# Attention, a routed mixture and a second MLP on one core: another placement for staged weight loads, conversions split into steps, another order at the end of attention

## The chip, the cores and the metric

The kernel runs on one core of a Trainium2 chip. The metric is device time in microseconds (us) of one execution; lower is better. The core's engines are TensorE (PE; its weight loads are shown apart as PEld), VectorE (DVE), ScalarE (ACT), GpSimd (POOL) and SyncE (SP), which here only issues transfers. Each engine works through its own instructions in order; an instruction that waits holds back all that stand behind it on that engine.

## The reference

Three stages, all in float32. Attention looks back over a window of 64 positions; its output goes through a mixture of 8 experts, of which each row uses the one with the largest logit (rows with a skip score of 0 or less pass through unchanged); the result goes through a second MLP with 2048 inner columns.

```python
scores = scale * q @ k.T                      # q, k, v: [4, 8, 576, 64]
mask = (rel >= 0) & (rel < 64)                # rel = pos[:, None] - pos[None, :]
attn = softmax(where(mask, scores, -1e9))
x = (attn @ v) laid out as [2304, 512]

do_compute = x @ w_skip > 0
logits = x @ w_gate                           # 8 experts
gate = softmax(logits) at the largest logit
x = x + gate * (relu(x @ w1[e]) @ w2[e])      # w1: [8, 512, 1024], w2: [8, 1024, 512]

h = x @ w_in                                  # w_in: [512, 2048], w_out: [2048, 512]
g = where(h >= 1, h, where(h <= -1, 0, (h + 1) ** 2 / 4))
out = g @ w_out
```

## The kernel before

A matrix product in full precision is made of three products of halves: every operand is split into a rounded upper half and a remainder, and three of the four cross products are summed. So each weight has to be loaded (a **raw** tile), split by ACT (copy of the upper half) and by DVE or POOL (subtraction, `split_pair`, L120), and kept in a ring of 14 pairs of split weights. A raw tile is 512 KB. The weights of the second MLP come in another number format (`in_wd`, 64-bit words); five DVE operations turn a raw tile of it into float32 first (`convert_ops`, L127: shift, two or-with-mask operations, the magnitude, a compare-and-multiply), and two converted tiles (half pairs) make one pair to split. Some are converted early (`EARLY`, kept in the pools `early` and `earlier`), the others (`LATE`, 24 half pairs) during the second MLP.

**Raw loads.** All raw loads stand in one list, `to_load`, in the order in which they are used. `load_raws` (L96) starts as many as there is room for: at most `most[0]` in flight, in three pools of 4, 2 and 2 places (the third exists from the experts on). It takes the last pool that has room, `room[-1]`. `load_raws` is called whenever a split or a conversion has taken a raw tile, so a new load often gets the place of the tile that was just taken, and its transfer waits until the engine that reads that tile is done. Raw loads are issued by SP, between its other loads.

**Attention.** 18 tiles of 128 rows go through a loop over `t` (L557), software-pipelined: `stage_v(t-3)` (probabilities times values, PSUM tile `o`; then DVE makes `den`, `rec`, `x`), `stage_t(t-2)` (transposes `pt`, copied to `pts`), `stage_s(t)` (scores `s`, from q and k; DVE `nb`, ACT `pr`), the routing of earlier tiles (`stage_l2`, `stage_l`, `stage_x` with the transposes `px`, and `route_a` to `route_c` for groups of three tiles), then from the third iteration on one split on POOL, and raw loads. `stage_v(t)` also issues the two value loads (`vt`, 130 KB each) that `stage_v(t+2)` reads; odd iterations load 512 KB each of q and k; each tile of the result is stored to `x1` (256 KB) by ACT's queue. In iterations 5 and 8 a whole conversion stands at the end of the iteration (L589). The tiles still in the pipeline after the loop are finished by hand-ordered calls (L601 to L637).

**Experts.** For each of the 8 experts one or more tiles of 128 rows are gathered, go through `ffn` and are stored back. Weights are split and converted in hooks between the matmuls.

**Second MLP.** 96 steps; step k runs `stage_h` (matmuls `h`, 12 of 384 columns, for one block of 128 inner columns) and, two steps behind, `stage_o` (matmuls `po`, 9 of 512 columns). The step's DVE and ACT work makes `gs` from `h`. `bring_at` says in which step which half pair of `LATE` is converted (between the step's own DVE operations); a pair is split at the end of the step after its second half (`split_whole`). `prep_block` transposes the input rows of a block (`p2x`) and splits them into `x2T`. Two half pairs are converted ahead of step 0 (`AHEAD_OF_IT`). Before:

```python
bring_at = {}
for n in range(AHEAD_OF_IT, len(LATE)):
    bring_at[n - AHEAD_OF_IT if n < 8 else 6 + (n - 8) * 7 // 5] = n
```

Of the kernel before, what the change touches and what calls it, by code (L numbers as in the profile page):

```python
# [10 lines left out]
F32 = mybir.dt.float32  # L11
F32R = mybir.dt.float32r
BF16 = mybir.dt.bfloat16
I32 = mybir.dt.int32
# [5 lines left out]
P = 128  # L20
# [9 lines left out]
NT = N // P  # L30
# [21 lines left out]
)  # L52
AHEAD_OF_IT = 2

# [10 lines left out]
def moe_chain(  # L65
# [30 lines left out]
    def load_raws(eng=nc.sync):  # L96
        while to_load and len(raws) < most[0]:
            used = [n for _, n in raws.values()]

            last = to_load[0] in LATE  # L100
            room = [n for n in range(1 if last else len(rawp)) if used.count(n) < RAWS[n]]
            if not room:
                return
            u, c = to_load.pop(0)
            at = rawp[room[-1]]
            if u < U_IN:
                r = at.tile([P, 2, 512], F32, tag="raw", name=f"raw{u}_{c}")
                eng.dma_start(r, wu[u, :, c : c + 2])
            else:
                r = at.tile([P, 512, 2], I32, tag="raw", name=f"raw{u}_{c}")  # L110
                eng.dma_start(
                    r.rearrange("p n w -> p (n w)").bitcast(I64), wd[u - U_IN, :, c]
                )
            raws[u, c] = r, room[-1]

# [39 lines left out]
    def do_split(u, c, eng):  # L155
        split_pair(u, c, raws.pop((u, c))[0] if u < U_IN else early.pop((u, c)), ring, eng)
        load_raws()

    def do_convert(u, c, into):
        if c % 2 == 0:  # L160
            early[u, c] = into.tile([P, 2, 512], F32, tag="early", name=f"c{u}_{c}")
        convert(early[u, c // 2 * 2][:, c % 2].bitcast(I32), raws.pop((u, c))[0])
        load_raws()

    def work(todo, engines):
# [82 lines left out]
    with ExitStack() as actx:  # L248
# [79 lines left out]
        def stage_t(t):  # L328
            for g in (2 * t, 2 * t + 1):
# [4 lines left out]
                pts = ap2.tile([P, 4, P], F32, tag="pts", name=f"pts{g}")  # L334
                if g % 2 == 0:
                    nc.scalar.activation(pts, pt, AF.Copy)
# [213 lines left out]
        nc.scalar.dma_start(x1[N : N + 1, :].rearrange("o (p c) -> (o p) c", p=27), zero)  # L550
        load_raws()
        of = {}
        for j, n in enumerate(ROUTES):
            t0 = len(of)
            of.update({t0 + i: (t0, i, n, j % 2) for i in range(n)})
        due, since = {}, {}
        for t in range(NT):  # L557
            if t >= 3:
# [10 lines left out]
            if t >= 3:  # L569
                store_t(t - 3, nc.scalar)  # L570
            if t >= 5:
                stage_l2(t - 5, *of[t - 5][1:])
# [14 lines left out]
            for f in due.pop(t, ()):  # L587
                f()
            if t in (5, 8):  # L589
                work(converts, [dve])  # L590

            if splits and since.get(splits[0][1:], t) + 2 <= t:
                work(splits, [pool])
            load_raws()
            for key in raws:
# [3 lines left out]
        t0 = t1 - ROUTES[-2]  # L599
        later = [f for g in sorted(due) for f in due[g]]  # L600
        stage_v(NT - 3)  # L601
        store_t(NT - 3, nc.scalar)
        stage_t(NT - 2)
        stage_l2(NT - 5, *of[NT - 5][1:])
        stage_l(NT - 4)
        stage_x(NT - 3)
        stage_t(NT - 1)
        stage_v(NT - 2)
        store_t(NT - 2, nc.sync)
        stage_l2(NT - 4, *of[NT - 4][1:])  # L610
        route_a(t0, of[t0][2])
        stage_l(NT - 3)
# [3 lines left out]
        end["lg"] = psp.tile([P, 4, P], F32, tag="pt0", name="lg_end")[:, 0, 0 : n * (NE + 1)]  # L616
        end["rk"] = psp.tile([P, 4, P], F32, tag="pt1", name="rk_end")
        stage_l2(NT - 3, *of[NT - 3][1:])
        for f in later:
# [15 lines left out]
        route_c(t1, n)  # L635
        work(converts, [dve] * len(converts))
        work(splits, [pool] * len(splits))  # L637
# [163 lines left out]
    with ExitStack() as fctx:  # L801
# [25 lines left out]
        def stage_h(xT, nb, m, k):  # L827
            turn[0] ^= 1
            ph = bank(6 + turn[0], [P, TB], f"h2_{nb}_{m}")
            n = 0  # L830
            for c in range(KD):
                for a, b in PASSES:
                    nc.tensor.matmul(  # L833
                        ph, lhsT=halves[U_IN + m // 4, c][:, b, (m % 4) * P : (m % 4 + 1) * P],
                        rhs=xT[:, a, c, :], start=(n == 0), stop=(n == 3 * KD - 1),
                    )
                    n += 1

# [62 lines left out]

        bring_at = {}
        for n in range(AHEAD_OF_IT, len(LATE)):
            bring_at[n - AHEAD_OF_IT if n < 8 else 6 + (n - 8) * 7 // 5] = n
        first = ring.tile([P, 2, 2, 512], F32, tag="pair", name="c_first")
# [3 lines left out]
        def half_pair(n):  # L909
# [7 lines left out]
            r = raws[u, c][0]  # L917
            mag = fp.tile([P, 512], F32, tag="mag", name=f"mag{u}_{c}")
            ops = convert_ops(cws[n // 2][:, c % 2].bitcast(I32), r, mag)
            return ops, [partial(nc.scalar.activation, mag, r[:, :, 1].bitcast(F32), AF.Abs)]  # L920

        def done(n):
            raws.pop(LATE[n])
            load_raws()
# [27 lines left out]
        xs = {0: load_block(0, nc.sync)}  # L952

        most[0] = RAWS[0] - 1
        load_raws()
# [24 lines left out]
        for k in range(len(steps) + LAG):  # L980
# [9 lines left out]
            if k >= LAG:  # L990
# [9 lines left out]
                if k < len(steps):  # L1000
                    stage_o(pos[v], gss.pop(k - LAG), m, m0, m1)
                    if m == KF - 1:
                        finish(pos[v], nb, rest=rest if v == 5 else None)
                    if HF + LAG <= k + 1 < HF + LAG + NTT:
                        put_aside(pos[0], k + 1 - HF - LAG)
# [66 lines left out]
```

## Time and profile before

| | us |
|---|---|
| median of 3 runs | 749.52 (745.4 to 752.06) |
| profiled execution, its time | 744.33 |
| its span, first to last instruction | 742.6 |
| mean granted TensorE clock in it | 0.98 of full speed |
| PE busy, of the span | 682.9 (92%) |
| DVE busy | 432.9 (58%) |
| ACT busy | 382.3 (51%) |
| POOL busy | 95.1 (13%) |

Busy shares are means over three unlike stages. Attention runs to about 146 us, the experts from there to about 306 us, the second MLP to the end. A time in brackets behind an instruction in the timeline is the idle time of its engine just before it, with what ended it. PE times in a timeline show the clock too: the same group of matmuls takes longer when the granted clock is low.

### The profile page before, as it was taken

How to read it: one execution, taken by the hardware profiler on the slowest of the kernel's cores; microseconds unless marked ns; L12 is line 12 of the kernel's file. 1: busy time of each engine (PE TensorE's matmuls, PEld its weight loads, DVE VectorE, ACT ScalarE, POOL GpSimd, SP SyncE). 2: the span in 40 equal slices, each digit the busy share in tenths (PEclk: the TensorE clock that was granted, in tenths of full speed). 3: DMA queues.
4: the chain of work that ended last, by engine and by line, in shares of the span. 5: the costliest groups of instructions: out<-in, count | busy, mean ns of one | idle time of the engine just before them, and what ended most of it. 6: DMA issues, size and time to landing. Idle time of an engine off the chain costs nothing.

```text
span 742.6 us, 12124 instructions
## 1 busy us (share of the span) xinstructions
PE 682.9 (92%) x4605; PEld 581.4 (78%) x4605; DVE 432.9 (58%) x851; ACT 382.3 (51%) x761; POOL 95.1 (13%) x96
## 2 busy tenths in 40 slices
PE   7677887789798999799899999999999999999997
PEld 6565666667676777488798998999998998998995
DVE  4477776649759159679888874434343443333332
ACT  5654663027456257356676665545444544445443
POOL 2335554322022122100000000000000000000000
PEclk9987999999999999999999999999999999999999
DMA  8896965158949348354242400202030021002001
GB/s 262 261 280 199 288 197 144 31 172 265 334 134 350 115 126 297 135 172 142 87 142 86 128 1 0 72 15 72 15 86 1 1 44 43 1 0 44 1 1 43
DMA packets 34502, 88.81 MB, mean 120 GB/s; under 512 B 6958, under 2 KB 8110, under 8 KB 34420
## 3 DMA queue, kind: packets, MB, share of 16 engines
q1 hardware_dynamic: 26208, 74.34, 32.5%
q10 hardware_dynamic: 5892, 6.83, 2.8%
q0 software_dynamic: 2320, 6.58, 2.7%
q8 instruction: 47, 0.77, 0.4%
q14 instruction: 35, 0.29, 0.1%
HBM read 75.65 MB, written 13.12 MB: 120 GB/s over the span
## 4 chain that ended last, share of the span: by engine, by line
PE 47%; DVE 7%; DMA 3%; issue 2%; ACT 2%; ACTq 0%; POOLq 0%; DVEq 0%; SPq 0%
PE po L862 23%; PE h L833 23%; DVE c L855 2%; DMA x<-mx,idx 2%; ACT q L845 1%; DVE gs L853 1%; DVE w L123 1%; DVE c L852 1%; PE p2x L824 1%; DMA mx<-x,idx 1%; DVE q L844 1%; DVE x2T L118 0%; DVE q L848 0%; PE spare L946 0%; DVE c_first L855 0%
## 5 line engine op out<-in xcount | busy, mean ns | idle before, releaser
L833 PE MATMUL h<-x2T,w 128*128 128x384 f32 x1152 | 218.2, 337 | 4.3 <-ACT x2T L117 2.2
L862 PE MATMUL po<-w,gs 128*128 128x512 f32 x864 | 217.4, 395 | 0.7 <-DVE w L123 0.6
L833 PEld LDWEIGHTS h<-x2T,w 128*128 128x128 f32 x1152 | 204.6, 188 | 13.6 <-DVE x2T L118 2.7
L862 PEld LDWEIGHTS po<-w,gs 128*128 128x128 f32 x864 | 159.5, 188 | 31.2 <-DVE w L123 1.3
L841 ACT ACTIVATE q<-h 128x384 f32<-128x384 f32 x96 | 47.0, 489 | 109.7 <-PE h L833 108.3
L844 DVE TENSOR_SCALAR q<-q 128x384 f32<-128x384 f32 x96 | 34.3, 358 | 99.9 <-ACT q L841 99.6
L848 DVE TENSOR_TENSOR q<-hs,q 128x384 f32<-128x384 f32 x96 | 53.6, 559 | 49.5 <-ACT q L845 49.5
L850 ACT ACTIVATE gs<-q 128x384 fp32r<-128x384 f32 x96 | 50.4, 525 | 60.0 <-DVE q L848 60.0
L853 DVE TENSOR_TENSOR gs<-q,gs 128x384 fp32r<-128x384 f32 x96 | 53.6, 558 | 43.8 <-ACT gs L850 43.8
L720 PE MATMUL y<-w,hT 128*128 128x512 f32 x264 | 69.3, 402 | 4.9 <-DVE hT L118 4.9
L122 ACT ACTIVATE w<-raw 128x1024 fp32r<-128x1024 f32 x64 | 65.4, 1063 | 14.1 <-PEq L779 3.6
L845 ACT ACTIVATE q<-q 128x384 f32<-128x384 f32 x96 | 50.5, 526 | 23.3 <-DVE q L844 20.1
L720 PEld LDWEIGHTS y<-w,hT 128*128 128x128 f32 x264 | 47.7, 188 | 17.4 <-DVE hT L118 8.4
L123 DVE TENSOR_TENSOR w<-raw,w 128x1024 fp32r<-128x1024 f32 x50 | 58.9, 1218 | 2.6 <-ACT w L122 1.6
L323 ACT ACTIVATE pr<-s,nb 128x128 f32<-128x128 f32 x144 | 39.1, 386 | 29.4 <-DVE nb L319 29.4
L843 ACT ACTIVATE hs<-h 128x384 f32<-128x384 f32 x96 | 46.8, 488 | 0.0
L123 POOL TENSOR_TENSOR w<-raw,w 128x1024 fp32r<-128x1024 f32 x14 | 33.4, 2387 | 62.1 <-ACT w L122 62.1
L682 PE MATMUL ha<-w,mxT 128*128 128x512 f32 x132 | 34.0, 404 | 7.8 <-DVE mxT L118 3.3
L348 PE MATMUL o<-vt,pts 128*64 128x65 f32 x576 | 27.0, 250 | 12.4 <-DMA vt<-in_vs 11.1
L682 PEld LDWEIGHTS ha<-w,mxT 128*128 128x128 f32 x132 | 23.8, 188 | 17.1 <-DVE mxT L118 4.1
L348 PEld LDWEIGHTS o<-vt,pts 128*64 128x64 f32 x576 | 23.6, 160 | 16.3 <-DMA vt<-in_vs 10.8
L682 PE MATMUL hb<-w,mxT 128*128 128x512 f32 x132 | 35.0, 401 | 0.0
(159 smaller groups left out, 702.4 us busy)
## 6 DMA issues: line engine op xcount, KB each, us to landing
raw<-in_wu SPq DMA_DIRECT2D x62, 512.0 KB, 6.4
raw<-in_wd SPq DMA_DIRECT2D x32, 512.0 KB, 4.3
x<-x SPq DMA_DIRECT2D x20, 256.0 KB, 3.3
x<-x ACTq DMA_DIRECT2D x19, 256.0 KB, 5.8
vt<-in_vs SPq DMA_DIRECT2D x36, 130.0 KB, 5.6
out<-out SPq DMA_DIRECT2D x36, 128.0 KB, 2.4
q<-in_qs SPq DMA_DIRECT2D x8, 512.0 KB, 7.4
kt<-in_ks SPq DMA_DIRECT2D x8, 512.0 KB, 8.4
```

What stands on the lines that cost most here:

```text
L122: nc.scalar.activation(t[:, 0], src, AF.Copy)
L123: eng.tensor_tensor(t[:, 1], src, t[:, 0].bitcast(F32), ALU.subtract)
L348: nc.tensor.matmul(o[k * BLK : (k + 1) * BLK, h, 0:VW], lhsT=pts[k][:, h // 2, half * BLK : (half + 1) * BLK], rhs=vt[(2 * t + k) % B][:, ...
L682: nc.tensor.matmul(ph, lhsT=xT[:, a, c, :], rhs=halves[4 * e + j, c][:, b, :], start=(n == 0), stop=(n == len(seq) - 1),)
L720: nc.tensor.matmul(py, lhsT=hT[j][:, a, c, :], rhs=halves[4 * e + 2 + j, c][:, b, :], start=(j == 0 and c == 0 and (a, b) == PASSES[0]), s ...
L833: nc.tensor.matmul(ph, lhsT=halves[U_IN + m // 4, c][:, b, (m % 4) * P : (m % 4 + 1) * P], rhs=xT[:, a, c, :], start=(n == 0), stop=(n == ...
L841: nc.scalar.activation(q, ph, AF.Relu, bias=0.5, scale=0.5)
L845: nc.scalar.activation(q, q, AF.Square)
L848: nc.vector.tensor_tensor(q, h, q, ALU.max)
L850: nc.scalar.activation(gs[:, 0], q, AF.Copy)
L853: dve.tensor_tensor(gs[:, 1], q, gs[:, 0].bitcast(F32), ALU.subtract)
L862: nc.tensor.matmul(po[i], lhsT=gs[:, a, i * P : (i + 1) * P], rhs=w[:, b, :], start=(m == m0 and (a, b) == PASSES[0]), stop=(m == m1 - 1 a ...
```

## The change

- `load_raws` picks, of the pools with room, the one from which a tile was taken longest ago (`left`, `take_raw`), no longer the last.
- No raw load stands ahead of the attention loop, and none in its iteration 0.
- The two conversions inside the loop are cut into their ten operations, two in an iteration from iteration 6 on (`convert_by_parts`): one before `stage_l2`, one behind the routing.
- After the loop, `stage_t(16)` goes ahead of `stage_v(15)`, `stage_t(17)` ahead of `stage_x(15)`, `route_a` of tiles 12 to 14 behind `stage_v(17)`; one store goes from ACT's queue to SP's; one `pts` copy goes from ACT to DVE.
- Three half pairs, not two, are converted ahead of the second MLP; for the first two the magnitude is written into a part of the ring (`first`), no longer into a new tile of the pool `fp`. The others come in steps 0, 1, 3, 4, 6, and from step 8 on three in four steps (before: one in each of steps 0 to 8, then five in seven).
- Up to four raw loads are in flight at the start of the second MLP, three from step 6 (before: three from the start). In step 0 the matmuls that read the upper half of x come first.

```diff
-AHEAD_OF_IT = 2
+AHEAD_OF_IT = 3
@@ load_raws
             u, c = to_load.pop(0)
-            at = rawp[room[-1]]
+            n = min(reversed(room), key=lambda n: left.get(n, 0))
+            at = rawp[n]
...
-            raws[u, c] = r, room[-1]
+            raws[u, c] = r, n
+
+    left = {}
+
+    def take_raw(key):
+        r, n = raws.pop(key)
+        left[n] = max(left.values(), default=0) + 1
+        return r
...
+    def convert_by_parts(todo, into):
+
+        for _, u, c in todo:
+            if c % 2 == 0:
+                early[u, c] = into.tile([P, 2, 512], F32, tag="early", name=f"c{u}_{c}")
+            for op in convert_ops(early[u, c // 2 * 2][:, c % 2].bitcast(I32), raws[u, c][0]):
+                yield
+                op()
+            take_raw((u, c))
+            load_raws()
@@ stage_t
-                if g % 2 == 0:
+
+                if g % 2 == 0 and t + 2 != NT:
                     nc.scalar.activation(pts, pt, AF.Copy)
@@ the attention loop
-        load_raws()
...
+        parts = convert_by_parts(converts, earlyp)
         for t in range(NT):
...
                 store_t(t - 3, nc.scalar)
+            if t >= 6:
+                next(parts, None)
             if t >= 5:
                 stage_l2(t - 5, *of[t - 5][1:])
...
-            if t in (5, 8):
-                work(converts, [dve])
+            if t >= 6:
+                next(parts, None)
...
-            load_raws()
+            if t:
+                load_raws()
...
+        stage_t(NT - 2)
         stage_v(NT - 3)
-        store_t(NT - 3, nc.scalar)
-        stage_t(NT - 2)
+        store_t(NT - 3, nc.sync)
         stage_l2(NT - 5, *of[NT - 5][1:])
         stage_l(NT - 4)
+        stage_t(NT - 1)
         stage_x(NT - 3)
-        stage_t(NT - 1)
         stage_v(NT - 2)
...
-        route_a(t0, of[t0][2])
         stage_l(NT - 3)
...
+        route_a(t0, of[t0][2])
         stage_l2(NT - 3, *of[NT - 3][1:])
@@ the second MLP
+            seq = [(c, a, b) for c in range(KD) for a, b in PASSES]
+            if k == 0:
+                seq.sort(key=lambda z: z[1])
...
+        bring_at = {0: 3, 1: 4, 3: 5, 4: 6, 6: 7}
+        for n in range(8, len(LATE)):
+            bring_at[8 + (n - 8) * 4 // 3] = n
...
+            if n < 2:
+
+                mag = first[:, 1, n]
+            else:
+                mag = fp.tile([P, 512], F32, tag="mag", name=f"mag{u}_{c}")
...
-        most[0] = RAWS[0] - 1
         load_raws()
...
+                    if k == 6:
+
+                        most[0] = RAWS[0] - 1
```

What stands in the engines' rows, at three places. First SP, from the first loads of q and k to the loads of iteration 5 (`raw0_0` is the raw tile of unit 0, first pair; `vt0` to `vt3` are the four value tiles, `kt` the keys). Before:

```order
L108 DMA raw0_0_244<-in_wu 128x1024
L108 DMA raw0_2_246<-in_wu 128x1024
L270 DMA q2_317<-in_qs 128x1024
L274 DMA kt_148<-in_ks 128x1024
L108 DMA raw1_0_371<-in_wu 128x1024
L108 DMA raw1_2_373<-in_wu 128x1024
L279 DMA vt0_149<-in_vs 64x520
L279 DMA vt1_150<-in_vs 64x520
L270 DMA q3_449<-in_qs 128x1024
L274 DMA kt_148<-in_ks 128x1024
L111 DMA raw32_0_463<-in_wd 128x512
L279 DMA vt2_151<-in_vs 64x520
```

And with the change, the same stretch:

```order
L290 DMA q2_313<-in_qs 128x1024
L294 DMA kt_148<-in_ks 128x1024
L110 DMA raw0_0_316<-in_wu 128x1024
L110 DMA raw0_2_318<-in_wu 128x1024
L110 DMA raw1_0_368<-in_wu 128x1024
L299 DMA vt0_149<-in_vs 64x520
L299 DMA vt1_150<-in_vs 64x520
L290 DMA q3_444<-in_qs 128x1024
L294 DMA kt_148<-in_ks 128x1024
L110 DMA raw1_2_458<-in_wu 128x1024
L299 DMA vt2_151<-in_vs 64x520
```

The first raw loads moved behind the load of `q2`, and one raw load fewer stands ahead of the first `vt0`. Before, `raw1_0` takes the place of `raw0_0`, `raw32_0` that of `raw0_2`, `raw32_1` that of `raw1_0`; with the change these three and `raw1_2` all get places that nothing has used yet, `raw2_0` and `raw2_2` the places of `raw0_0` and `raw0_2`. From iteration 8 on all six places are taken in both kernels, and most loads get the place of the tile whose split was issued in the same iteration.

Second DVE, the end of iteration 5 and the start of iteration 6 before (`c_0` is the converted tile, `xT` the copy of the transposes `px`):

```order
L393 COPY ls_642<-misc 128x128
L374 COPY xT_649<-px_644 128x512
L153 TENSOR_SCALAR c_0_651<-raw_0_463 128x512
L153 SCALAR_TENSOR_TENSOR c_0_651<-raw_0_463,c_0_651 128x512 x2
L153 TENSOR_SCALAR raw_0_463<-raw_0_463 128x512
L153 SCALAR_TENSOR_TENSOR c_0_651<-raw_0_463,c_0_651 128x512
L355 TENSOR_SCALAR den_681<-o_664 128x8
```

With the change, the end of iteration 6 and iteration 7 up to its routing:

```order
L395 COPY xT_738<-px_733 128x512
L181 TENSOR_SCALAR c_0_725<-raw_0_550 128x512
L376 TENSOR_SCALAR den_765<-o_748 128x8
L378 RECIPROCAL rec_767<-den_765 128x8
L380 TENSOR_TENSOR x_769<-o_748,rec_767 128x512
L359 COPY pts_785<-pt_780 128x512
L339 TENSOR_REDUCE nb_808<-s_788 128x4
L339 TENSOR_REDUCE nb_810<-s_789 128x4
L181 SCALAR_TENSOR_TENSOR c_0_725<-raw_0_550,c_0_725 128x512
L414 COPY ls_832<-misc 128x128
```

Five operations in a row ahead of `den` have become one ahead of `den` and one between `nb` and `ls` in each iteration.

Third DVE, from the start of the second MLP to step 0 (`c_first` holds the first converted tiles, `x2T` the split input rows). Before:

```order
L959 SCALAR_TENSOR_TENSOR c_first<-mag_1_5892,c_first 128x512
L123 TENSOR_TENSOR w_0_5900<-c_first,w_0_5900 128x1024
L118 TENSOR_TENSOR x2T_5885<-p2x_0_5903,x2T_5885 128x4x128
L118 TENSOR_TENSOR x2T_5885<-p2x_1_5912,x2T_5885 128x4x128
L118 TENSOR_TENSOR x2T_5885<-p2x_2_5921,x2T_5885 128x4x128
L844 TENSOR_SCALAR q_0_5954<-q_0_5954 128x384
L847 TENSOR_SCALAR c_first<-raw_2_5138 128x512
```

With the change:

```order
L986 SCALAR_TENSOR_TENSOR c_first<-c_first 128x512
L986 TENSOR_SCALAR c_first<-raw_2_5138 128x512
L986 SCALAR_TENSOR_TENSOR c_first<-raw_2_5138,c_first 128x512 x2
L986 SCALAR_TENSOR_TENSOR c_first<-mag_2_5900,c_first 128x512
L132 TENSOR_TENSOR w_0_5908<-c_first,w_0_5908 128x1024
L127 TENSOR_TENSOR x2T_5885<-p2x_0_5911,x2T_5885 128x4x128
L127 TENSOR_TENSOR x2T_5885<-p2x_1_5920,x2T_5885 128x4x128
L127 TENSOR_TENSOR x2T_5885<-p2x_2_5929,x2T_5885 128x4x128
L869 TENSOR_SCALAR q_0_5962<-q_0_5962 128x384
L872 TENSOR_SCALAR c_first<-raw_3_5146 128x512
```

The third half pair (`raw_2`) moved from step 0 to a place ahead of the split and of `x2T`; step 0 now converts the fourth.

## Rows read from the trace of the kernel before

**Rows 1.** Stretches of 20 us: busy us of each engine, PEclk, DMA share, GB/s

```profile
40.00:60.00 20.00, 15.36 (x222) 11.71 (x219) 14.17 (x32) 9.15 (x25) 7.14 (x3) 0.83 1.00 297
...
120.00:140.00 20.00, 15.52 (x238) 12.36 (x230) 13.72 (x53) 3.79 (x12) 4.26 (x6) 0.91 0.27 79
...
340.00:360.00 20.00, 16.05 (x80) 13.69 (x79) 18.56 (x34) 12.99 (x27) 0.00 (x0) 1.00 0.37 118
...
400.00:420.00 20.00, 20.00 (x103) 18.21 (x102) 17.09 (x32) 12.23 (x25) 0.00 (x0) 1.00 0.26 79
```

**Rows 2.** Timeline of PE in attention: start, us, line, tile, count, idle before

```profile
15.99 1.24 PE L348 MATMUL o<-vt,pts 128*64 128x65 f32 x32 [0.16 <-issue]
...
20.89 1.15 PE L348 MATMUL o<-vt,pts 128*64 128x65 f32 x32
21.98 1.09 PE L333 MATMUL pt<-ident,pr 128*128 128x128 f32 x8
...
30.31 0.35 PE L348 MATMUL o<-vt,pts 128*64 128x65 f32 x2 [4.83 <-DMA vt<-in_vs]
30.95 1.97 PE L348 MATMUL o<-vt,pts 128*64 128x65 f32 x30 [0.30 <-DMA vt<-in_vs]
...
36.50 0.66 PE L372 MATMUL px<-ident,x 128*128 128x128 f32 x4
...
44.15 1.09 PE L372 MATMUL px<-ident,x 128*128 128x128 f32 x4 [2.52 <-DVE x L359]
45.16 2.00 PE L348 MATMUL o<-vt,pts 128*64 128x65 f32 x32
...
53.00 0.33 PE L348 MATMUL o<-vt,pts 128*64 128x65 f32 x2 [1.88 <-DMA vt<-in_vs]
...
54.73 1.97 PE L333 MATMUL pt<-ident,pr 128*128 128x128 f32 x8
...
68.92 1.09 PE L372 MATMUL px<-ident,x 128*128 128x128 f32 x4 [4.05 <-DVE x L359]
...
77.01 1.15 PE L348 MATMUL o<-vt,pts 128*64 128x65 f32 x32
```

**Rows 3.** Timeline of SP in attention: start, us, loads issued in a row

```profile
22.30 0.80 SPq L108 DMA_DIRECT2D raw<-in_wu  x2
23.19 1.11 SPq L279 DMA_DIRECT2D vt<-in_vs  x2
```

**Rows 4.** SP's waits from 0 to 130 us: line, releaser, total us, times, longest

```profile
SPq L108 <- POOL w L123: 22.9, 6, 5.2
SPq L111 <- POOL w L123: 14.8, 4, 6.9
```

**Rows 5.** Timelines of DVE and POOL around the two conversions in attention

```profile
38.45 1.42 DVE L153 SCALAR_TENSOR_TENSOR c<-raw,c 128x512 int32<-128x512 int32 x2
...
40.25 2.72 DVE L153 SCALAR_TENSOR_TENSOR c<-raw,c 128x512 f32<-128x512 f32 x1
...
63.22 3.45 DVE L153 SCALAR_TENSOR_TENSOR c<-raw,c 128x512 int32<-128x512 int32 x2
...
39.92 2.50 POOL L123 TENSOR_TENSOR w<-raw,w 128x1024 fp32r<-128x1024 f32 x1 [9.03 <-ACT w L122]
```

**Rows 6.** Timeline of PE after the attention loop

```profile
132.37 0.42 PE L385 MATMUL misc<-xT,wg_sb 128*32 128x128 f32 x8 [1.84 <-DVE d L416]
```

**Rows 7.** PE's waits from 320 to 400 us: total us, times, longest

```profile
PE h L833 <- ACT x2T L117: 2.2, 1, 2.2
PE h L833 <- DVE x2T L118: 2.0, 2, 1.1
PE po L862 <- DVE w L123: 0.6, 1, 0.6
```

**Rows 8.** The chain that ended last, start of the second MLP: start, us, what

```profile
319.34 1.77 PE spare L946 x5
321.12 2.12 PE h L833 x12
```

More of the change, by code (lines that the diff above doesn't have):

```diff
@@ L155, in do_split @@
     def do_split(u, c, eng):
-        split_pair(u, c, raws.pop((u, c))[0] if u < U_IN else early.pop((u, c)), ring, eng)
+        split_pair(u, c, take_raw((u, c)) if u < U_IN else early.pop((u, c)), ring, eng)
         load_raws()
@@ L161, in do_convert @@
             early[u, c] = into.tile([P, 2, 512], F32, tag="early", name=f"c{u}_{c}")
-        convert(early[u, c // 2 * 2][:, c % 2].bitcast(I32), raws.pop((u, c))[0])
+        convert(early[u, c // 2 * 2][:, c % 2].bitcast(I32), take_raw((u, c)))
         load_raws()
+    def convert_by_parts(todo, into):
[7 more added lines that the diff above has]
+            load_raws()
     def work(todo, engines):
@@ L635, in moe_chain @@
         route_c(t1, n)
-        work(converts, [dve] * len(converts))
+        for _ in parts:
+            pass
         work(splits, [pool] * len(splits))
@@ L829, in stage_h @@
             ph = bank(6 + turn[0], [P, TB], f"h2_{nb}_{m}")
[L830 to L837, printed above, removed]
+            seq = [(c, a, b) for c in range(KD) for a, b in PASSES]
+            if k == 0:
+                seq.sort(key=lambda z: z[1])
+            for n, (c, a, b) in enumerate(seq):
+                nc.tensor.matmul(
+                    ph, lhsT=halves[U_IN + m // 4, c][:, b, (m % 4) * P : (m % 4 + 1) * P],
+                    rhs=xT[:, a, c, :], start=(n == 0), stop=(n == 3 * KD - 1),
+                )
             fill, mags, ends = bring(k)
@@ L900, in moe_chain @@
         part = dram.tile([TB, DM], F32, name="part")
-        bring_at = {}
-        for n in range(AHEAD_OF_IT, len(LATE)):
-            bring_at[n - AHEAD_OF_IT if n < 8 else 6 + (n - 8) * 7 // 5] = n
+        bring_at = {0: 3, 1: 4, 3: 5, 4: 6, 6: 7}
+        for n in range(8, len(LATE)):
+            bring_at[8 + (n - 8) * 4 // 3] = n
         first = ring.tile([P, 2, 2, 512], F32, tag="pair", name="c_first")
@@ L917, in half_pair @@
             r = raws[u, c][0]
-            mag = fp.tile([P, 512], F32, tag="mag", name=f"mag{u}_{c}")
+            if n < 2:
+                mag = first[:, 1, n]
+            else:
+                mag = fp.tile([P, 512], F32, tag="mag", name=f"mag{u}_{c}")
             ops = convert_ops(cws[n // 2][:, c % 2].bitcast(I32), r, mag)
@@ L922, in done @@
         def done(n):
-            raws.pop(LATE[n])
+            take_raw(LATE[n])
             load_raws()
```

## The prediction

> **What bounds the kernel now.** I read the stretches of 20 us first: where is PE not full, and at what clock? From 400 us on it is busy 20.00 of 20 us at full clock; there nothing of this change can win or lose. In the second MLP's first 80 us it falls to 16.05 of 20 while DVE stands at 18.56, so DVE sets the pace; in attention it is at 15.36, at a mean granted clock of 0.83, with the transfers at a share of 1.00 [rows 1].
>
> In PE's timeline of attention the reader is to see that a good iteration of the loop is short and few are good. From `o` at 15.99 to `o` at 20.89 it takes 4.90 us. The next seven, up to 77.01, take 56.12, where seven of 4.90 would be 34.3: 21.8 us too much [rows 2]. The brackets say why. Twice PE waits for value loads, 4.83 and 1.88 us, and twice for DVE's `x`, 2.52 and 4.05 us; and after each such wait the same groups take nearly twice as long (`o` 1.97 or 2.00 for 1.15, `pt` 1.97 for 1.09, `px` 1.09 for 0.66), as at 1.2 instead of 2.4 GHz [rows 2].
>
> Who holds the value loads? SP's timeline shows two raw loads at 22.30 and the two `vt` loads behind them at 23.19, though `stage_v` of that iteration, whose end frees the `vt` tile, ended at 17.2 (15.99 + 1.24) [rows 2, 3]. SP's list of waits names the blocker: raw loads waited 22.9 + 14.8 = 37.7 us in ten waits for POOL's split of the tile whose place they take [rows 4]. Who holds `x`? The conversions, of which one operation took 2.72 us, where two of its kind took 1.42 together, beside a split on POOL [rows 5].
>
> The expert stage loses its time to orders that the change leaves as they are; its splits, conversions and matmuls stand in the same order on PE, DVE, ACT and POOL, and only the places of its raw tiles are dealt out differently. I cost it at nothing; the cover is that transfers run far ahead of it (share 0.27 from 120 to 140 us) [rows 1], and if that is gone the head start is lost there (second rival).
>
> **Part 1, raw loads.** In iterations 2 to 7 the loads now get places that are fresh or were left iterations ago, so SP no longer stands at POOL there. What that frees: the waits of 4.83 and 1.88 us, and the slow groups right behind them, 1.97 − 1.15 = 0.82 and 1.97 − 1.09 = 0.88 [rows 2]: 8.4 us. From iteration 8 on all six places are taken, and loads wait for the split of their own iteration as before; I count nothing there. The raw loads that no longer stand ahead of the loop start about an iteration later, and each split with them; the splits still end inside the loop.
>
> **Part 2, conversions by steps.** The two lumps cost PE 2.52 and 4.05 us of waiting, and in slow groups 1.09 − 0.66 = 0.43 and 2.00 − 1.15 = 0.85 behind the first, and behind the second the same two and a `pt` of 1.97 − 1.09 = 0.88, as behind the wait at 53.00 [rows 2]: 10.0 us. Nothing of the work goes away: ten operations of up to 0.7 us remain, two in an iteration. What hides them is DVE's own idle time: even in the stretch with the first lump it is busy 14.17 of 20 us [rows 1]. Queued behind the one that stands ahead of `den` are `den`, `rec`, `x`, and PE's `px` behind those; about 2.0 us of lateness is free there, since the 4.5 us of the first lump from 38.45 to 42.97 made PE wait only 2.52 [rows 2, 5]. Without that cover each step would cost up to its two operations, 1.4 us.
>
> Parts 1 and 2 together would give 18.4 of the 21.8 us. But a second limit comes next: the transfers. In the seven iterations from the one at 20.89 on the changed kernel moves 11 raw tiles of 512 KB, three loads each of q and k of 512 KB, 14 value loads of 130 KB and 7 stores of 256 KB, together 12.6 MB (5.77 + 3.15 + 1.86 + 1.83). At the 297 GB/s that a full stretch showed [rows 1] that is 42.4 us, so these iterations can hardly fall below 42.4 from 56.1: at most 13.7 of the 18.4 us. Value loads queue behind raw loads in such traffic, so some waits stay. I take **11 us**, with ends of 4 (only the first wait goes, and little else) and 18 (part of the raw traffic runs over into later iterations, where the share falls).
>
> A rule of the skill speaks against part 2, and the trace shows its effect. The row: the operation of 2.72 us began at 40.25, while POOL's subtraction ran from 39.92 to 42.42; before POOL began, two such operations took 1.42 [rows 5]. The Trainium skill, "SBUF — State Buffer", section "SBUF: two separate sides", says that VectorE and GpSimd share a pair of ports as an exclusive lock, and that a VectorE operation with two inputs in SBUF fully blocks while a GpSimd operation that reads SBUF holds it; here it agrees with the row. By that rule six of the ten operations (those that read the raw tile or the magnitude and the converted tile) can each be held, at six moments instead of two; this is the third rival.
>
> **Part 3, the end of attention.** Now PE waits 1.84 us because `route_a` (started at its `d`) stands ahead of the copy `ls` on DVE [rows 6]; the new order puts it behind the last `stage_v`. The transposes moved up let their copies run while PE does `o`; the copy that goes from ACT to DVE adds one copy to DVE's queue, with `den` and PE's next `px` behind it. The group behind the wait ran slow too (0.85 at most, from `o` in attention). `route_a` itself is not gone, its operations now delay the last `ls`. Between 0 and 2.7 us; I take **2**, near the row's own wait. The store moved to SP's queue stands behind nothing but value loads; zero.
>
> **Part 4, the second MLP.** PE's waits from 320 to 400 us are 2.2 + 2.0 us for `x2T` and 0.6 us for a split, 4.8 in all [rows 7]. They come from one half pair converted in each of steps 0 to 8 with DVE at 18.56 of 20 [rows 1]; with one half pair ahead of step 0 and five in the first eight steps, these steps lose a third of their conversions, and from step 8 on three in four steps is about the old rate (five in seven) with other neighbours. So 4.8 us go. One split becomes late anew: the pair for inner block 6 is split at the end of step 7 and read in step 8, where before a whole step lay between; I price that at the one such wait that the trace has, 0.6 [rows 7]. Net **4.2 us**, between 2.5 and 5. The start itself gains nothing: PE's own keep-warm matmuls end at 321.12, and `h` follows at once [rows 8], so an earlier `x2T` and the reordered matmuls of step 0 find PE busy. The third half pair sits in the wait for the last stores of the experts, where DVE has nothing else; had it no room there, its four operations, 2.8 us (4 × 0.71 [rows 5]), would come ahead of `x2T`. Raw loads, one more of them in flight, stand behind the first block's x loads on SP.
>
> **Sum.** 11 + 2 + 4.2 = 17.2 us off the profiled execution of 744.33 (span 742.6 and 1.7 around it): 727.1. That execution was below the median of the runs, 749.52; off the median it is **732.3**, and I forecast 732.
>
> **The rivals.** *The transfers take it back.* With the stalls gone the raw loads, splits and value loads crowd into less time, and the waits for `vt` return one after another, from iteration 8 on more than now. For it: the share of 1.00 [rows 1] and the unchanged placement from iteration 8. Against: 120 to 140 us has a share of 0.27, so there is room to run over [rows 1]. Price: the loop keeps 4 us: 749.5 − 4 − 2 − 4.2 = 739.3.
>
> *The experts absorb the head start.* They begin 13 us earlier, but their first raw tiles may not be there, and ACT's splits wait for them. Against it is that idle share just before they begin [rows 1]. It would leave part 4 only: 745.3, within 1%.
>
> *Slower: the lock between DVE and POOL.* Place: iterations 6 to 11, each with two conversion operations and one split on POOL. If both of an iteration were held to 2.72 us each, 5.4 us of lateness against the 2.0 that is free makes a PE wait of 3.4, and slow groups of 0.43 + 0.85 + 0.88 = 2.2 behind it [rows 2, 5]: 5.6 in each of five iterations, 28. Against that stand the 10.0 of the two lumps, some 5 of part 1, 2 and 4.2: 749.5 + 28 − 21.2 = 756.3. It decides when four of the five iterations meet it (4 × 5.6 = 22.4). Against: one held operation in an iteration costs 2.72 − 2.0 = 0.7 and no more, and of the trace's six such operations two were held, one in each lump (2.72, and 3.45 for a pair) [rows 5].
>
> **How the numbers follow.** Forecast, gains of 11 to 22 us (727 to 738): 0.62. More than that, the loop at its bound of 18 and the other parts at theirs (down to 721): 0.06. Transfers, around 739 (738 to 742): 0.18. Experts, 742 to 747: 0.09. Lock, above 747: 0.05. The range 721 to 744 leaves out the last and about half of the one before. Faster by over 1%, which is about what a measurement of this kernel can tell (its three runs spread 0.9%), means below 742.0: 0.86; within 1%: 0.09; slower: 0.05.
>
> **What the changed profile would show.** Part 1: SP's waits of raw loads for POOL fall from 37.7 us to about half, and the wait for `vt` of 4.83 is gone. Part 2: no wait of PE for `x` above 1 us in the loop; the granted clock from 40 to 60 us rises above 0.83. The iteration that starts at 77.01 now starts near 66. Part 3: no wait of 1.84 us for `d`. Part 4: waits for `x2T` gone, one for a split of about 0.6, PE full from about 325 less the head start. The forecast is wrong if the loop's iterations stay near 8 us with the transfers at a share of 1.00, if held conversion operations pile up, or if the experts' first tiles wait for raw loads.

## Result, and the profile after

The median is 737.42 us (20 runs, 729.69 to 743.4) against 747.13 us (20 runs) for the kernel before on the same chips: a ratio of 0.9875, interval 0.9853 to 0.9897, 9.3 us less. The time lies in the range and the direction is right; the gain is little more than half of the 17.2 us forecast. The profiled execution took 739.42 us (span 737.7). It lies 2.0 us above its median, and that of before 2.8 us below the median of these runs, so stretches of the two profiles must be compared with their scatter in mind. One kernel of the study (POOL issues, with the new end) has its profile from a disturbed execution; it is left out below, and its two successors stand for it.

The windows of 20 us that answer to [rows 1] (columns as there):

```profile
20.00:40.00 20.00, 18.74 (x341) 14.49 (x340) 14.17 (x32) 15.88 (x43) 7.11 (x3) 1.00 1.02 320
40.00:60.00 20.00, 15.88 (x252) 12.01 (x252) 16.33 (x48) 12.83 (x34) 9.07 (x6) 0.90 1.05 265
...
340.00:360.00 20.00, 17.40 (x88) 14.92 (x87) 15.50 (x29) 12.35 (x25) 0.00 (x0) 1.00 0.34 105
```

From 20 to 60 us the transfers now stand at a share above 1.00; from 340 to 360 DVE fell from 18.56 to 15.50 and PE rose from 16.05 to 17.40. PE's timeline of attention, as in [rows 2]: the same iterations start at

```profile
21.92 1.15 PE L369 MATMUL o<-vt,pts 128*64 128x65 f32 x32
...
44.77 0.33 PE L369 MATMUL o<-vt,pts 128*64 128x65 f32 x2 [1.95 <-DMA vt<-in_vs]
...
65.53 1.45 PE L369 MATMUL o<-vt,pts 128*64 128x65 f32 x32
...
85.75 0.33 PE L369 MATMUL o<-vt,pts 128*64 128x65 f32 x2 [1.21 <-DMA vt<-in_vs]
...
105.54 1.53 PE L369 MATMUL o<-vt,pts 128*64 128x65 f32 x32 [1.52 <-DMA vt<-in_vs]
```

The iteration that started at 77.01 starts at 65.53 (forecast: near 66), and the seven iterations ahead of it take 43.6 us, not 56.1. The six behind it take 40.0 us (65.53 to 105.54), where before they took 37.2 (77.01 to 114.20). SP's waits for POOL tell the same story, split at that iteration, first after, then before (columns as in [rows 4]; the rows ahead of the dots are the earlier stretch):

```profile
SPq L110 <- POOL w L132: 4.8, 2, 2.8
...
SPq L110 <- POOL w L132: 15.6, 4, 7.0
SPq L113 <- POOL w L132: 7.5, 2, 5.0
```

```profile
SPq L108 <- POOL w L123: 11.2, 3, 5.2
SPq L111 <- POOL w L123: 0.3, 1, 0.3
...
SPq L111 <- POOL w L123: 14.6, 3, 6.9
SPq L108 <- POOL w L123: 6.7, 2, 4.0
```

In the earlier stretch they fell from 11.5 to 4.8 us; in the later one they stayed, 21.3 and 23.1. SP's largest wait of the earlier stretch before, which the prediction left out, was another one, for DVE; with the change it fell as well (before, then after):

```profile
SPq L108 <- DVE rec L357: 14.8, 2, 8.9
```

```profile
SPq L110 <- DVE rec L378: 3.2, 1, 3.2
```

The two waits before ended at 42.99 and 67.77, as the two conversions ended (42.97 and 67.74; the view names `rec`, which stands right behind them on DVE): each time a raw load was to take the place of the tile that was being converted. The conversions, grouped by form as busy us and mean ns, answer to [rows 5]:

```profile
L181 DVE SCALAR_TENSOR_TENSOR c<-raw,c 128x512 int32<-128x512 int32 x4 | 2.9, 717 | 0.0
L181 DVE SCALAR_TENSOR_TENSOR c<-raw,c 128x512 f32<-128x512 f32 x2 | 1.4, 682 | 0.0
```

None was held. Before:

```profile
L153 DVE SCALAR_TENSOR_TENSOR c<-raw,c 128x512 int32<-128x512 int32 x4 | 4.8, 1200 | 0.1
L153 DVE SCALAR_TENSOR_TENSOR c<-raw,c 128x512 f32<-128x512 f32 x2 | 3.4, 1706 | 0.1
```

At the end of attention the wait of 1.84 us for `d` [rows 6] is gone, and others stand in its place, in PE's timeline:

```profile
118.59 0.66 PE L393 MATMUL px<-ident,x 128*128 128x128 f32 x4 [0.32 <-DVE x L380]
121.75 0.43 PE L406 MATMUL misc<-xT,wg_sb 128*32 128x128 f32 x8 [1.10 <-DVE xT L395]
122.79 0.66 PE L393 MATMUL px<-ident,x 128*128 128x128 f32 x4 [0.61 <-DVE x L380]
126.16 0.53 PE L537 MATMUL misc<-at,to 128*128 128x144 f32 x3 [1.31 <-DVE mine L439]
```

In the second MLP, PE's waits from 320 to 400 us, as [rows 7], are 2.6 us for 4.8:

```profile
PE h L859 <- DVE x2T L127: 0.9, 1, 0.9
PE po L887 <- ACT w L131: 0.9, 1, 0.9
PE po L887 <- DVE w L132: 0.8, 1, 0.8
```

As in [rows 8], the chain still passes from PE's own keep-warm matmuls to `h`, so an earlier `x2T` alone would find PE busy. Ahead of them it holds a load of the x rows, which took 5.93 us here and 2.55 before, so rows that came earlier would have moved the start:

```profile
309.29 5.93 DMA x<-x
...
315.26 1.11 PE p2x L849 x4
316.38 2.13 PE spare L975 x5
318.51 6.47 PE h L859 x36
```

### The profile page after: what moved, and what is told of

It is laid out like the page before. It is cut to its first block, busy times and chain, and to the rows that moved or that the text cites. A ratio compares the mean times of both kernels' runs of the same rounds, so it can differ in the third digit from the quotient of the medians.

```text
span 737.7 us, 12121 instructions
## 1 busy us (share of the span) xinstructions
PE 687.6 (93%) x4605; PEld 583.9 (79%) x4605; DVE 429.5 (58%) x852; ACT 382.2 (52%) x760; POOL 96.2 (13%) x96
## 4 chain that ended last, share of the span: by engine, by line
PE 52%; DVE 4%; ACT 1%; DMA 1%; issue 1%; SPq 0%; ACTq 0%; DVEq 0%
PE h L859 25%; PE po L887 25%; PE p2x L849 1%; DVE c L880 1%; DVE c_first L986 1%; DMA x<-x 1%; DVE c L877 1%; ACT q L870 1%; DVE w L132 0%; DVE gs L878 0%; DVE q L869 0%; PE spare L975 0%; DVE x2T L127 0%; ACT q L866 0%; DVE q L873 0%
## 5 line engine op out<-in xcount | busy, mean ns | idle before, releaser
L875 ACT ACTIVATE gs<-q 128x384 fp32r<-128x384 f32 x96 | 50.4, 525 | 60.0 <-DVE q L873 60.0
L870 ACT ACTIVATE q<-q 128x384 f32<-128x384 f32 x96 | 50.5, 526 | 22.3 <-DVE q L869 18.8
L343 ACT ACTIVATE pr<-s,nb 128x128 f32<-128x128 f32 x144 | 39.2, 383 | 24.3 <-DVE nb L339 24.3
L707 PE MATMUL ha<-w,mxT 128*128 128x512 f32 x132 | 37.0, 432 | 7.2 <-ACT mxT L126 3.9
L707 PEld LDWEIGHTS ha<-w,mxT 128*128 128x128 f32 x132 | 26.3, 207 | 17.3 <-ACT mxT L126 5.0
L127 DVE TENSOR_TENSOR hT<-hTp,hT 128x512 fp32r<-128x512 f32 x22 | 15.1, 689 | 36.3 <-ACT hT L126 28.8
L339 DVE TENSOR_REDUCE nb<-s 128x4 f32<-128x512 f32 x36 | 23.1, 684 | 17.9 <-PE s L332 13.5
```

The source lines that it names most:

```text
L707: nc.tensor.matmul(ph, lhsT=xT[:, a, c, :], rhs=halves[4 * e + j, c][:, b, :], start=(n == 0), stop=(n == len(seq) - 1),)
L870: nc.scalar.activation(q, q, AF.Square)
L875: nc.scalar.activation(gs[:, 0], q, AF.Copy)
```

## Experiments

Times of the thirteen kernels are compared by their ratio to the kernel before on the same chip; 0.001 is 0.75 us, and an interval reaches 0.002 to 0.006 to either side. The stretches are read from PE's timeline of each profile: "4 to 11" from the `o` of iteration 4 to that of iteration 11 (20.89 to 77.01 before), "11 to 17" from there to the `o` of iteration 17, "end" from there to the last keep-warm group of attention, "first tile" from there to the next expert's transposes `mpx`.

| kernel | 4 to 11 | 11 to 17 | end | first tile | ratio [interval] |
|---|---|---|---|---|---|
| before | 56.1 | 37.2 | 31.5 | 15.9 | 1 |
| changed | 43.6 | 40.0 | 30.2 | 19.7 | 0.9875 [0.9853, 0.9897] |
| without part 1 | 49.2 | 41.6 | 31.8 | 18.8 | 0.9986 [0.9953, 1.0018] |
| without part 2 | 48.9 | 39.2 | 31.3 | 18.8 | 0.9883 [0.9853, 0.9914] |
| without part 3 | 44.6 | 43.0 | 30.8 | 16.5 | 0.9835 [0.9808, 0.9863] |
| without part 4 | 42.9 | 37.9 | 33.6 | 16.5 | 0.9925 [0.9898, 0.9951] |
| part 1 alone | 45.4 | 41.3 | 32.8 | 18.7 | 0.9878 [0.9836, 0.9921] |
| part 2 alone | 50.7 | 41.3 | 30.8 | 15.9 | 0.9998 [0.9964, 1.0033] |
| part 3 alone | 55.9 | 37.0 | 31.1 | 21.4 | 1.0014 [0.9981, 1.0047] |
| old end, MLP start mended | 45.4 | 42.6 | 30.3 | 21.0 | 0.9858 [0.9816, 0.9899] |
| half the raw bytes | 39.5 | 42.6 | 32.1 | 17.5 | 0.9848 [0.9790, 0.9905] |
| POOL issues | | | | | 0.9820 [0.9766, 0.9873] |
| POOL issues, old end | 41.7 | 39.0 | 31.1 | 15.8 | 0.9798 [0.9748, 0.9848] |
| the same, more keep-warm | 41.4 | 38.7 | 28.8 | 16.1 | 0.9790 [0.9747, 0.9834] |

**Without part 1.**

```diff
-            n = min(reversed(room), key=lambda n: left.get(n, 0))
+            n = room[-1]
...
+        load_raws()
         of = {}
...
-            if t:
-                load_raws()
+            load_raws()
```

> The changed kernel with the raw loads placed and started as before (last place with room; loads ahead of the loop and in iteration 0); the rest stays changed. If the terms of the loop add up (theory A: of the 12 us that the loop gained, 8.4/18.4, some 5.5, are the placement's), the waits for value loads of about 5 and 2 us return and the time is 4 to 6 us above the changed kernel's 737.4. If the transfers bind whichever of the two remedies is made (theory B), one alone gives nearly all of it: 0 to 2 us above. In the trace the first iteration after the raw loads shows which: a wait for vt of over 4 us in A, under 2 in B.

Measured: 0.9986; all but 1.0 of the 9.3 us is lost, more than theory A's 4 to 6. The wait for value loads at the third `o` is back in PE's timeline, at a size between the two marks of that text:

```profile
30.73 0.48 PE L369 MATMUL o<-vt,pts 128*64 128x65 f32 x2 [3.53 <-DMA vt<-in_vs]
```

**Without part 2.** The two conversions stand whole in iterations 5 and 8 again.

```diff
-            if t >= 6:
-                next(parts, None)
...
+            if t in (5, 8):
+                work(converts, [dve])
```

> The changed kernel with the two conversions whole again, at the end of iterations 5 and 8. Theory A: 10.0/18.4 of 12, some 6.5 us, are lost, less what is given back later anyway: 5 to 7 us above 737.4, with PE waits for x of about 2.5 and 4 us. Theory B: the transfers leave room for little else, 0 to 2 us above.

Measured: 0.9883, 0.6 us above the changed kernel: theory B's size. Yet the waits for `x` are all back:

```profile
42.56 1.08 PE L393 MATMUL px<-ident,x 128*128 128x128 f32 x4 [3.63 <-DVE x L380]
...
64.53 1.09 PE L393 MATMUL px<-ident,x 128*128 128x128 f32 x4 [4.06 <-DVE x L380]
```

They cost time where they stand (48.9 us for the seven iterations), and part of it comes back in the six behind (39.2). PE's waits for `vt` are not more than in the changed kernel, 5.0 us.

**Without part 3, and without part 4.** The calls after the loop in their old order, with the `pts` copy on ACT; and in the second MLP, two half pairs ahead, the old `bring_at`, three raw loads in flight, no sorting.

```diff
-        stage_t(NT - 2)
         stage_v(NT - 3)
-        store_t(NT - 3, nc.sync)
+        store_t(NT - 3, nc.scalar)
+        stage_t(NT - 2)
...
+        route_a(t0, of[t0][2])
         stage_l(NT - 3)
```

> The changed kernel with the old order after the loop. The prediction's own term: 2 us above 737.4, with the wait for d of 1.8 us back. By the two traces (the stretch from o of tile 15 to idx takes 21 to 22 us in both): 0, from -1 to 1.

> The changed kernel with the second MLP's part as before: two half pairs ahead, the old table of steps, three raw loads in flight at its start, the old order of matmuls in step 0. The prediction's term: 4.2 us above 737.4. By the two traces the changed steps gained 2.3 and the changed start lost some 2: then it is 0 to 1 us above, with h starting about 2 us earlier relative to the end of the experts and waits for x2T of about 4 us back.

Measured without part 3: 0.9835, 3.0 us faster than with it (by the two intervals 2.6 us to either side), though the wait for `d` is back at its old size:

```profile
127.23 0.43 PE L406 MATMUL misc<-xT,wg_sb 128*32 128x128 f32 x8 [1.84 <-DVE d L437]
```

Without part 4: 0.9925, 3.7 us slower (also 2.6 to either side); the prediction's term of 4.2 holds, and the reading of the two traces (0 to 1) fails. The waits behind `h` come back:

```profile
PE h L858 <- ACT x2T L126: 2.2, 1, 2.2
PE h L858 <- DVE x2T L127: 1.4, 2, 1.1
PE po L887 <- DVE w L132: 0.6, 1, 0.6
```

**Parts alone on the kernel before.** Each is the changed kernel with the edits above that take out the other three.

> The kernel before with part 1 alone (places left longest ago, no raw load ahead of the loop). Theory B, which the first four runs suggest: once SP is free, the transfers bind the loop, and the lumps cost nothing. Then the seven iterations between the o that starts the fifth of the loop and the one seven later take 43 to 45 us as in the changed kernel, though PE waits 2.5 and 4 us for x, and the time is 8 us below the kernel before (ratio about 0.989). Theory A, terms that add: 56.1 - 8.4 = 47.7 us for the seven, 5.5 us below before (0.993).

> The kernel before with part 3 alone (the new order after the loop). By the prediction's term 2 us below before (0.997). By the run that took part 3 out of the changed kernel, where the time fell by 3 us: 3 us above (1.004), with the stretch from the end of attention to the experts' second tile longer, at a low granted clock. If that fall was the scatter of two medians, 0 (1.000, within 0.002).

> The kernel before with part 2 alone (conversions two operations a step). The prediction's term for it, alone, was 10.0 us (ratio 0.987). By the run with parts 2 to 4 and the old placement (seven iterations in 49.2 us, the later six in 41.6 where the kernel before takes 37.2, ratio 0.9986 with part 4 worth some 4 us in it): the seven iterations shorten by 6 to 8 us, the later ones, which now hold the conversions, give back about 4, and the time is 0 to 3 us below before (0.996 to 1.000). If one half pair's operations are held by POOL's splits, single operations take 2.7 us and the time is above before.

Measured: part 1 alone 0.9878, as much as the whole change; part 2 alone nothing (0.9998); part 3 alone 1.0 us slower (1.0014), which the interval does not tell from nothing. Theory B, that either remedy alone wins nearly all, holds for part 1 and falls with part 2 and with the run without part 1. With part 1 alone PE waits 2.8 and 4.06 us for `x`, and the seven iterations take 45.4 us. Part 2 alone shortens them to 50.7, and the `vt` waits that it leaves go on behind:

```profile
32.46 2.41 PE L369 MATMUL o<-vt,pts 128*64 128x65 f32 x32 [3.90 <-DMA vt<-in_vs]
...
74.25 0.48 PE L369 MATMUL o<-vt,pts 128*64 128x65 f32 x2 [3.70 <-DMA vt<-in_vs]
```

**Half the raw bytes.** The eight loads and their splits:

```diff
-                eng.dma_start(r, wu[u, :, c : c + 2])
+                if 6 <= raws_n[0] <= 14:
+                    r = r[:, 0:1]
+                    eng.dma_start(r, wu[u, :, c : c + 1])
+                    r = r.to_broadcast([P, 2, 512])
```

> The changed kernel, but the seventh to fourteenth raw load fetch only the first half of their tile, 256 KB, and the splits read that half twice; engines have the same work, the transfers less, and the result is another one. Seven of these loads, 1.84 MB, fall into the seven iterations that took 43 to 45 us in seven kernels with the new placement. If transfers bind those, they shorten by 1.84 MB at 288 GB/s, 6.4 us, to 36.5 to 39 us. If it is PE (busy 36 to 38 us of them) and DVE that bind them by now, they stay at 42 to 45, and the total within 1 us of the changed kernel.

The "seven kernels" of this text were six: the one without part 2 took 48.9. Measured: 39.5 us, against 42.9 to 45.4 in the four kernels that have parts 1 and 2 and load by SP (mean 44.1). So 4.6 of the 6.4 us went with the bytes, by one profile, and not because SP stood less: its waits for POOL in the stretch are 6.8 us, 4.8 in the changed kernel. The row of the stretch then shows PE at full clock and a transfer share of 0.87 for 1.02 in the changed kernel:

```profile
23.83:63.29 39.46, 34.24 (x620) 26.32 (x619) 32.12 (x85) 28.99 (x77) 19.90 (x13) 1.00 0.87 263
```

```profile
21.92:65.53 43.61, 38.23 (x619) 29.46 (x619) 32.52 (x84) 29.03 (x76) 21.46 (x13) 0.92 1.02 288
```

The next six iterations took 42.6 us, against a mean of 40.9 in the four, and gave 1.7 us of it back. The ratio, 0.9848, is 2.0 us better than the changed kernel's, less than the intervals can tell.

**POOL issues the raw loads that follow its splits** (in the loop only), and with it the old end.

```diff
+                by[0] = pool
                 work(splits, [pool])
+                by[0] = nc.sync
@@ do_split
-        load_raws()
+        load_raws(by[0])
```

> The changed kernel, but inside the loop the raw loads that follow a split are issued by POOL, which has just made that split, so SP stands for none of them. If SP's 31.7 us of waits for POOL still hold value loads back, PE's waits for vt (5.4 us up to 112 us) fall below 2 and the time is 3 us or more below 737.4. If the transfers bind, the loop's first seven iterations stay at 43 to 45 us and the time within 1 us. If issuing costs POOL so much that splits come late: 2 us above.

> The changed kernel with POOL issuing the raw loads behind its splits in the loop, and the old order after the loop. If the later iterations give back some 4 us because SP stands at POOL's splits, the stretch from iteration 11's o to iteration 17's stays near 38 us, as with POOL issuing and the new end, and the ratio to the kernel before is 0.978 to 0.982. If that run's lead was scatter: 0.984 to 0.988.

Measured: 0.9820 and 0.9798, 4.1 and 5.7 us below the changed kernel. In the second, SP waits for PE to leave the value tiles, no longer for POOL, in the six later iterations:

```profile
SPq L300 <- PE o L370: 20.7, 6, 5.6
```

and these take 39.0 us, the seven before them 41.7; the four kernels with parts 1 and 2 and loads by SP have means of 40.9 and 44.1. PE's waits for `vt` there add up to 2.0 us, of 5.4 in the changed kernel:

```profile
63.37 0.33 PE L370 MATMUL o<-vt,pts 128*64 128x65 f32 x2 [1.62 <-DMA vt<-in_vs]
64.10 1.12 PE L370 MATMUL o<-vt,pts 128*64 128x65 f32 x30 [0.41 <-DMA vt<-in_vs]
```

So the first branch of the text on POOL's issues came true, nearly to its numbers (waits for `vt` below 2 us, the time 3 us or more below): SP's waits still held value loads back. Both stretches are shorter, by 2.4 and 1.9 us.

**The second MLP's start mended, with the old end.**

```diff
-        bring_at = {0: 3, 1: 4, 3: 5, 4: 6, 6: 7}
+        bring_at = {0: 3, 1: 4, 2: 5, 4: 6, 5: 7}
...
-        load_raws()
         for n in range(AHEAD_OF_IT):
...
-            done(n)
+            take_raw(LATE[n])
...
+        load_raws(nc.scalar)
         xs[1] = load_block(1, nc.scalar)
```

> The changed kernel with the old order after the loop, and two changes in the second MLP: the raw loads at its start are issued by ACT behind the first block's x2T, not by SP beside the x loads, and half pairs 5 and 7 are converted in steps 2 and 5, one step earlier, so that their pairs are split two steps ahead of use. If the loads sharing the way are what made x late, the third x load lands within 3.2 us (5.9 in the changed kernel), h starts some 2 us earlier relative to the experts' last store, and the two waits for the split (1.7 us) go: 2 to 3 us below the same kernel without these two changes (733.6), 731. If the lost time was elsewhere: 733 to 734. If raw loads now come too late for step 1: 735 or more.

Measured: 0.9858, no gain over 0.9835 without the two edits; that theory falls, though no x load behind the first is waited for any more. The waits for the split are gone, but those for `x2T` grew, to 2.7 us from 1.8 without the two edits, and with no raw load beside them the x rows still found PE at low clock (`p2x` 1.08 for 0.63):

```profile
PE h L859 <- ACT x2T L126: 1.9, 1, 1.9
PE h L859 <- DVE x2T L127: 0.8, 1, 0.8
...
314.96 1.08 PE L849 MATMUL p2x<-ident,x 128*128 128x128 f32 x4 [3.43 <-DMA x<-x]
```

**More keep-warm matmuls.**

```diff
-KEEP = (24, 26, 56, 6, 8, 28)
+KEEP = (24, 26, 86, 6, 8, 34)
```

> The same as the kernel with POOL issuing and the old end, with more of PE's own keep-warm matmuls: 86 for 56 ahead of the first gathered rows, 34 for 28 ahead of the second MLP. If the lost time at both starts is the low clock behind PE's waits of 2.4 to 3.9 us for the gathered rows and 1.4 to 3.5 us for the input rows, ha takes 3.05 us (4.5 to 5.5 in most runs) and h follows the experts' last store by 11 us or less (12.3 to 13): 2 to 3 us below its twin. If the rows come as late and the clock falls all the same, or the matmuls themselves stand in the way: 0 to 2 us above.

Measured: 0.9790, not to be told from its twin's 0.9798; the predicted 2 to 3 us did not show in the medians. In the profile the wait for the gathered rows is down to 0.30 us and `ha` runs at full clock:

```profile
130.63 4.98 PE L421 MATMUL spare<-ones 128*128 128x128 bf16 x86
135.91 0.63 PE L693 MATMUL mpx<-ident,mx 128*128 128x128 f32 x4 [0.30 <-PE spare L421]
137.35 3.05 PE L710 MATMUL ha<-w,mxT 128*128 128x512 f32 x12 [0.81 <-ACT mxT L127]
```

but the twin's profile had `ha` at 3.05 as well, and `h` starts 13.0 us behind the experts' last `y` matmul, 12.7 in the twin. These two are the fastest kernels of the study, about 15 us below the kernel before and 6 below the changed one.

## Why the prediction was right, and where its sizes were off

The mechanism held in the main: SP, standing at another engine with value loads behind it, cost the early iterations their time, and the placement freed it. The prediction named POOL's splits alone. They held SP ahead of the wait of 4.83 us; ahead of the wait of 1.88 us SP stood 5.9 us for the first conversion, to 42.99, and issued the value loads at 46.45. So 2.8 of the 8.4 us of part 1 (that wait and the slow `pt` behind it) hung on a conversion, not on a split. The sum was too large in two of its terms.

That the time itself came so near, 737.4 for 732, is in part luck: the forecast was counted from a median of three runs, 749.52, and the twenty runs have 747.13. The time lies just inside the bracket "gains of 11 to 22 us", the gain of 9.3 does not.

**The loop, forecast 11 (ends 4 and 18).** Iterations 4 to 17 take 93.3 and 92.9 us in the two kernels with neither part (before, part 3 alone) and 83.6, 87.6, 80.8 and 88.0 in the four with both and SP loading, mean 85.0: about 8 us gained. Of its steps:
- Part 1, 8.4: alone it won 9.1 us, and taking it out lost 8.3. In the two profiles with it and without part 2, iterations 4 to 17 took 86.7 and 88.1, 5.7 less than without either. By the times the term stands, but in part by luck: in the stretch for which it was worked out, seven iterations, part 1 alone won 10.7 us, and 4.1 came back in the six behind it, which the term did not count.
- Part 2, 10.0: alone 0.1 us, on top of part 1 0.6 by the medians (2.4 by the profiles). This is the step that was mis-sized. PE's waits for `x` were real and are gone, but time won there was handed on to the next wait. Alone, part 2 shortened the seven iterations by 5.4 us and lost 4.1 in the six behind, where PE still waits for `vt`, with the raw loads placed as before. For its small worth on top of part 1 the prediction had a reason, the transfers, and used it only as a cap on the sum. Its floor of 42.4 us for the seven iterations is about where kernels with both parts arrived (41.4 to 45.4), and fewer bytes made them shorter (39.5): shown as one bound among others, since only 4.6 of 6.4 us followed the bytes.
- What it left out is the stretch behind: "from iteration 8 on ... I count nothing there". Those six iterations became longer, 40.9 on average in the four kernels for 37.1. That is the first rival, in part: the loads placed after iteration 8 wait for the split of their own iteration, as before, and SP with them (23.1 us). The forecast that these waits fall "to about half" failed for the same reason (31.7 us in all, of 37.7). That SP's standing is the cause is supported by the kernels in which POOL issues those loads: 39.0 and 38.7 us, and 4 to 6 us less time. The stretch alone would not show it, since the four range from 37.9 to 43.0.

**Part 3, forecast 2 (0 to 2.7): nothing, probably a loss of 1 to 3.** The named wait of 1.84 us went, but `mine`, `xT` and `x` then made PE wait 1.31, 1.10 and 0.32 + 0.61. On DVE `x` stands behind two `pts` copies (from 116.21 for 1.29 us) and `xT` behind another (120.41); the prediction named the copy that it added there and gave it no price. The question of what is late next it answered with `ls` alone. Three pairs of kernels differ in this part: with the new order the times are 3.0 us higher (the changed kernel), 1.6 (POOL issuing) and 1.0 (part 3 alone); only the first is more than the intervals leave open. Where the loss would lie is suggested by the table, not shown: "end" and "first tile" together are 50.4 us on average in six profiles with the new order and 48.0 in seven with the old, and `ha`, the first expert's matmuls, ran at full clock in one of the six and in five of the seven. Two of the seven, with 51.5 and 51.3, look like the new order, so scatter is not ruled out.

**Part 4, forecast 4.2: 3.7 measured.** Its one new wait was priced at 0.6 and took 0.9 + 0.8, and 0.9 of the waits for `x2T` stayed, so the waits account for 2.2 us. From the first `h` to the end the five profiles with the old second MLP take 421.8 to 423.5 us and the eight with the new one 419.3 to 420.9, 2.6 less on average. That the start itself gains nothing held: from the experts' last `y` to `h` the means are 14.0 and 14.2 us.

**The experts, "at nothing".** The changed kernel's profile loses 3.8 us at the first tile (19.7 for 15.9), which made me suspect the raw tiles' new places. The table speaks against that: two kernels with the changed attention loop have 16.5, and 21.4 is reached with part 3 alone, in the old places. It is scatter, or the end's new order (above), with `ha` at 3.05 us in some profiles and 4.45 to 5.49 in others.

**The lock.** The third rival did not come. The Trainium skill ("SBUF — State Buffer", section "SBUF: two separate sides") lets a VectorE operation with two inputs in SBUF block fully against a GpSimd operation that reads SBUF. Where it met one, the trace agrees: in the kernel with POOL issuing and the old end, POOL's split ran from 62.02 for 2.33 us, and the conversion took

```profile
62.20 2.71 DVE L182 SCALAR_TENSOR_TENSOR c<-raw,c 128x512 int32<-128x512 int32 x1
```

for 0.68 elsewhere. But that was one of the six two-input operations there, and none in the changed kernel. In the nine profiles with the steps one such operation was held in six, for 1.62 to 3.13 us, and two in none; the price of 5.6 us in each iteration needed two in each.

Summed with these sizes: 8 − 2 + 3.7 is about 10, and 9.3 was measured.

## What to carry to other kernels

Load requests on an in-order queue should not stand behind a request that waits for another engine; place them so that the wait is over, or let the engine that ends the wait issue them. Two stalls of one loop need not be two terms of a sum: here one was worth its whole price whether the other stood or not, and the other next to nothing either way, with further waits close behind it. Put each in alone, and take each out of the whole, before adding them. A stretch that gets its work earlier can give time back further on with its instructions unchanged, so a gain should be followed to the next point where all engines meet, over several profiles.

## What was not expected of the hardware

Loads issued by POOL were cheap here: 16 raw loads of 512 KB took POOL 0.57 to 0.58 us each on average, and SP no longer stood for them. The Trainium skill ("SBUF — State Buffer", section "SBUF: two separate sides") warns that a DMA issued by GpSimd can starve while a VectorE operation in a two-port mode holds the port pair they share, and advises the ACT or SP queue. No issue in the run quoted took over 0.73 us, and the `in_wu` tiles landed in 8.7 us (median), where those issued by SP in the changed kernel took 9.7 (from 20 to 112 us), so that did not show; the queue that stood still cost more.

```profile
raw<-in_wu POOLq DMA_DIRECT2D x11, 512.0 KB, 8.7
```

The scatter of single profiles is larger than the whole effect of parts 2 to 4: with the same code in the loop, iterations 4 to 17 took from 80.8 to 88.0 us in four kernels.
